# Chunk 0 ranked by token tile, its first blocks behind 12 of 16 scatters, and another written order of the head

## The chip, the cores and the metric

The kernel runs on 1 core of one Trainium2 chip. The metric is the device time of one execution in microseconds, lower is better. The kernel before was run three times: 1276.65, 1286.84 and 1290.79 us, median 1286.84 us.

## The reference

A causal 7-tap convolution along the sequence, one softmax-normalised set of taps for each of 8 heads, is followed by a mixture of 8 experts in which every token goes to the one expert with the largest logit. The input is 8 x 3584 tokens of width 192; an expert is 192 -> 1024 -> 192 with a ReLU.

```python
w = exp(weight - max) ; w = w / (sum(w) + 1e-9)            # (8 heads, 7 taps)
x = einsum('hk,bskhg->bshg', w, unfold(pad(x)))            # causal, then (28672, 192)
xn, en = x / (|x| + 1e-6), expert_emb / (|expert_emb| + 1e-6)
logits = xn @ en.T / tau
expert_idx = argmax(logits, axis=1)
gate_w = softmax(logits)[expert_idx]
out[mask_e] = gate_w[mask_e, None] * (relu(x[mask_e] @ w1[e]) @ w2[e])
```

## The kernel before, in words

The 28672 tokens are cut into 16 chunks of 1792. A chunk lies in SBUF as 112 partitions by 16 token tiles: tile t holds 112 tokens in a row, one to a partition. A chunk passes these steps:

- `load_x` fetches it; eight `conv` matmul pairs make the heads and ScalarE copies each back (L434).
- `square` sums the squares of a token tile (ScalarE L443 or VectorE L446); `scales` and `factor` turn them into a power of two and a norm.
- `scaled` works on a quarter of the chunk (4 tiles): VectorE multiplies by the power of two (L507), ScalarE casts the high half to float16 (L512, L513). `rest` subtracts to get the low half (L519, L522).
- The rows are turned so that the width lies on the partitions: for chunks 0 and 1 with TensorE transposes (`flip`, copied by ScalarE at L562), for the others with DMA transposes of SBUF by `turn` (L722), four to a chunk.
- `logits` multiplies with the expert embeddings. `rank` takes the largest logit, and finds for each token its place in its expert's region of a DRAM buffer `rows_d`. `put` scatters one token tile a time with an indirect DMA from GpSimd (L728), 16 to a chunk.

In `rank` places run first along the tiles of a partition (the scan at L657), then over the partitions (the matmuls at L667 and L669). So the first 128 places of an expert are filled from all 16 tiles.

An expert block takes 128 to 512 rows of one expert from `rows_d` with two DMA transposes (`rows_of`, L858): 40 matmuls for the hidden layer (L1002), ScalarE's ReLU to float16 (L1006), VectorE's low half (L1008), 24 matmuls for each 128 rows of output (L1023), ScalarE's scaling by the gate (L1028), an indirect store from GpSimd (L1030). The weights of all experts are first loaded, measured by `trace` and `exponents` (L355, L358, L365), and split into a high half (`high`, ScalarE L388) and a low half (`low`, VectorE L392).

The program has two parts. The head prepares the weights, takes chunks 0 and 1 to their scatters, chunk 2 up to the turned rows, and runs eight first blocks of 128 rows, one of each expert, on rows of chunk 0. Its order is written out by hand in `HEAD`, a string of short words, each of which emits one step; the instructions of TensorE, VectorE, ScalarE and GpSimd are then chained in that order (in `run`, from L1153 on), and SyncE's queue follows the program too. The words that matter here: `0k1 0k2 0k3 0u` are the four parts of chunk 0's ranking, the last with its scatters; `2s1` and `2r1` are `scaled` and `rest` of quarter 1 of chunk 2; `T2` the four DMA transposes of chunk 2; `dh3`, `dl3` the high and low halves of a part of expert 3's weights; `z6p0 z6p1 z6o` the two halves of the hidden layer and the output of expert 6's first block, `z6m` its gate; `FA` and `FB` the loads of the first blocks' rows (`first_rows`); `hx1` a trace of expert 7's weights.

Behind the head a planner (`dispatch`, `steer`) mixes expert blocks with the routing of the further chunks. The first blocks of this part are the 256-row blocks of phase 2, which need all scatters of chunks 0 and 1; `fetch` loads three of them right behind the head, and its transposes follow the four of `T2` on SyncE's queue.

`first_rows` waits for the first 16 scatters:

```python
self.after(self.rows_of(e * self.cap, v, 128, NT), NT)
```

Of the kernel before, what the change touches and what calls it, by code (L numbers as in the profile page):

```python
# [12 lines left out]
F16 = mybir.dt.float16  # L13
F32 = mybir.dt.float32
BF16 = mybir.dt.bfloat16
I32 = mybir.dt.int32
AF = mybir.ActivationFunctionType
ALU = mybir.AluOpType
AX = mybir.AxisListType
# [7 lines left out]
E = 8  # L27
F = 1024
HALO = 16
TP = 112  # L30
NT = 16
CT = TP * NT
XD = 224
RW = 240
# [18 lines left out]
NACT = 3  # L53
PINS = 12
WARM = 14
TURN, RANK, GAP = 7.0, 10.0, 0.5
RAW = 2 * (2 * F + F * D // 128)
AREAS = (1, 2), (1, 1), (1, 0), (0, 1), (1, 1), (1, 0), (0, 1)
HEAD = ("0c2 0c1 0c7 0c3 0c0 0c5 0c6 0c4 0q1 0q5 0q4 0q7 ax1 0q2 0q6 ax2 ax3 0q0 ah3 "
# [12 lines left out]
AHEAD = 0.4  # L72
HALF = 3 * 2048
SETTLE = 6.0
# [32 lines left out]
class _Moe:  # L107
# [100 lines left out]
    def constants(self):  # L208
        nc, cp = self.nc, self.cp
        nc.gpsimd.memset(self.xtb[:].rearrange(  # L210
            "p h (a k t) -> p (h a) k t", k=4, t=TP)[:, :, 3, 0:HALO], 0.0)
        nc.gpsimd.memset(self.rows2[:, :, :, XD + 2:], 0)
        nc.gpsimd.iota(self.ids, pattern=[[TP, NT]], base=TP - 1,
                       channel_multiplier=-1)
        head = self.xr[:, 0:2048].bitcast(F32)
        self.idf, self.onef = head[:, 0:128], head[:, 128:256]
        make_identity(nc, self.idf)
        self.idh = head[:, 256:320].bitcast(F16)
        nc.vector.tensor_copy(out=self.idh, in_=self.idf)
        nc.gpsimd.memset(self.onef, 1.0)  # L220
        self.oneh = cp.tile([128, 128], F16, name="oneh")
        nc.gpsimd.memset(self.oneh, 1.0)

        self.lth = cp.tile([128, 128], F16, name="lth")
        nc.gpsimd.memset(self.lth, 1.0)
        nc.gpsimd.affine_select(
            out=self.lth, in_=self.lth, pattern=[[1, 128]], base=0,
            channel_multiplier=-1, compare_op=ALU.is_gt, fill=0.0)

        tmp = self.op.tile([128, D], F32, tag="y", name="tmp")[:, 0:2 * E + 64].bitcast(I32)  # L230
        e8i = tmp[0:TP, 0:E]
        nc.gpsimd.iota(e8i, pattern=[[-1, E]], base=E, channel_multiplier=0)
        self.e8 = cp.tile([TP, E], F32, name="e8")
        nc.vector.tensor_copy(out=self.e8, in_=e8i)

        self.rst = cp.tile([TP, E, NT], F32, name="rst")
        nc.gpsimd.memset(self.rst, 1.0)
        nc.gpsimd.memset(self.rst[:, :, 0:1], 0.0)

        rn = tmp[:, E:E + NJ]  # L240
        nc.gpsimd.iota(rn, pattern=[[128, NJ]], base=1, channel_multiplier=1)
        self.rn = cp.tile([128, NJ], F32, name="rn")
        nc.vector.tensor_single_scalar(out=self.rn, in_=rn, scalar=float(self.N),
                                       op=ALU.mult)

        cbi = tmp[:, E + 64:]
        nc.gpsimd.iota(cbi, pattern=[[self.cap, E]], base=0, channel_multiplier=0)
        self.cb = cp.tile([128, E], F32, name="cb")
        nc.vector.tensor_copy(out=self.cb, in_=cbi)

        self.start = cp.tile([128, E], F32, name="start")
        nc.vector.tensor_copy(out=self.start, in_=cbi)
# [366 lines left out]
    def rank(self, c, lg, f):  # L619
        nc, sp = self.nc, self.sp  # L620
        head = c < PICK[0]
# [12 lines left out]
        if head:  # L634
# [11 lines left out]
            out=l, in0=l, scalar=0.0, op0=ALU.is_equal,  # L646
            in1=self.e8[:].unsqueeze(1).to_broadcast([TP, NT, E]), op1=ALU.mult)
        nc.vector.tensor_reduce(out=m, in_=l, op=ALU.max, axis=AX.X)
        oh = sp.tile([TP, E, NT], F32, tag="eb", name="oh")
        te = lambda v: v.rearrange("p e t -> p t e")  # L650
        nc.vector.tensor_tensor(out=te(oh[:]), in0=l, in1=bt(m[:]),
                                op=ALU.is_equal)


        inc = self.lp.tile([TP, E, NT], F32, tag="ea", name="inc")
        fl = lambda v: v.rearrange("p e t -> p (e t)")
# [32 lines left out]
        if c and c + 1 in PHASES and c + 1 < self.nch:  # L689
            self.hand_out(c + 1)  # L690


    def put(self, step=None):
        if not self.pend:
# [60 lines left out]
            self.scatter(p[:, e:e + 1], z)  # L755


    def limits(self, c):
        nc, n = self.nc, PHASES[c]
        t = self.lp.tile([128, E], F32, tag="ph_t", name="ph_t")  # L760
        nc.vector.tensor_tensor(out=t, in0=self.cb, in1=self.start, op=ALU.subtract)
        lim = self.hp.tile([128, E, NJ], F32, tag="lim", name="lim")[:, :, 0:n // 128]
        sh = [128, E, n // 128]
        nc.vector.scalar_tensor_tensor(
            out=lim, in0=t[:].unsqueeze(2).to_broadcast(sh), scalar=-float(self.N),
            in1=self.rn[:, 0:n // 128].unsqueeze(1).to_broadcast(sh),
            op0=ALU.mult, op1=ALU.add)
        at = None
        if c > 1:
            at = self.hp.tile([1, E], I32, tag="at", name="at")  # L770
            nc.vector.tensor_copy(out=at, in_=self.start[0:1, :])
        nc.vector.scalar_tensor_tensor(
            out=self.start, in0=self.start, scalar=float(n), in1=self.cb,
            op0=ALU.add, op1=ALU.min)
        self.lims[c] = lim, at

# [93 lines left out]
    def first_rows(self, k):  # L870
        nc = self.nc
        if not k:
            self.mt0 = self.cp.tile([128, E, 2], I32, name="mt0")
            m = self.rows_d[0:128, XD:XD + 2]
            self.after([nc.sync.dma_start(out=self.mt0, in_=bass.AP(
                tensor=m.tensor, offset=m.offset,
                ap=[[RW, 128], [RW * self.cap, E], [1, 2]])).ins], NT)
            self.x0 = []
        for i in range(4):
            e = 4 * k + i  # L880
            v = self.xr[:, 2048 + e * 512:2048 + (e + 1) * 512].rearrange("p (k t) -> p k t", t=128)
            self.after(self.rows_of(e * self.cap, v, 128, NT), NT)
            self.x0.append(v)

    def masked(self, ids, lim, name, behind=None):
# [350 lines left out]
```

## Time and profile before

| what | value |
| --- | --- |
| median of three runs | 1286.84 us |
| the profiled execution's own time | 1291.4 us |
| its span, first to last instruction | 1289.7 us |
| mean granted TensorE clock | 0.954 |
| TensorE matmuls busy | 1151.0 us, 89% of the span |
| VectorE, ScalarE, GpSimd busy | 665.5, 604.3, 530.0 us |

The profile is one execution. PE is TensorE's matmuls, PEld its weight loads, DVE VectorE, ACT ScalarE, POOL GpSimd, SP SyncE, which does nothing but issue DMAs. A line such as L1002 is a line of the kernel before. In a timeline row the first number is the start in us from the span's first instruction, the second the length in us; a bracket gives the idle time ahead of it and what ended that. "Issue" is time in which an engine waited for nothing that the profile shows, "remote" a signal whose sender the profile can't name. A clock of 1.00 is the upper of TensorE's two levels (2.4 GHz), 0.50 the lower (1.2 GHz).

### The profile page before, as it was taken

Reading aid. Unit: us, or ns where it says so; the run is one execution under the profiler, and the core shown is the slowest. Engines: PE = TensorE matmul, PEld = TensorE weight load, DVE = VectorE, ACT = ScalarE, POOL = GpSimd, SP = SyncE. Lnnn points to the kernel's source line nnn. Section 1 sums busy time; section 2 is a strip of 40 time slices with the busy share of each in tenths; the row PEclk is TensorE's granted clock in tenths of the full one; section 3 lists DMA queues with packets and bytes.
Section 4 is the critical chain, followed back from the end, with each engine's and each line's share of the span. In section 5 each row is a group of like instructions: output and inputs, shape, how many; then the busy total and the mean of one; then the engine's idle time right before and its main releaser. Section 6 shows DMA issues by size and latency. Waiting matters only on the chain. (4 is left out here: it accounts for less than half of the span.)

```text
span 1289.7 us, 29765 instructions
## 1 busy us (share of the span) xinstructions
PE 1151.0 (89%) x11202; PEld 905.3 (70%) x11202; DVE 665.5 (52%) x1863; ACT 604.3 (47%) x1479; POOL 530.0 (41%) x551
## 2 busy tenths in 40 slices
PE   5774998798998989899998999868999999999997
PEld 3473877586876766677776777636787878778776
DVE  5973666366545365454654737434334344445543
ACT  5973566345545545456454645213434343333333
POOL 3544245544553455355454544574222222222222
PEclk8896999899998999899999999978999999999999
DMA  9955755874966864748577574432022213221210
GB/s 250 260 115 159 144 93 137 168 160 97 183 128 149 173 124 130 169 107 185 109 159 148 121 145 103 113 87 70 29 48 51 58 39 65 65 53 33 52 45 23
DMA packets 324793, 146.64 MB, mean 114 GB/s; under 512 B 266606, under 2 KB 315117, under 8 KB 324640
## 3 DMA queue, kind: packets, MB, share of 16 engines
q1 hardware_dynamic: 300976, 93.98, 37.5%
q0 software_dynamic: 23664, 50.68, 13.6%
q8 instruction: 89, 1.46, 0.5%
q14 instruction: 64, 0.52, 0.1%
HBM read 38.35 MB, written 51.05 MB: 69 GB/s over the span
## 5 line engine op out<-in xcount | busy, mean ns | idle before, releaser
L1008 DVE SCALAR_TENSOR_TENSOR work<-h_ps,work 128x384 f16<-128x384 f32 (+1 forms) x536 | 320.0, 606 | 457.0 <-ACT work L1006 389.4
L1023 PEld LDWEIGHTS <-work 128*128 128x128 f16 x5472 | 462.6, 99 | 100.5 <-issue 47.9
L1023 PE MATMUL o_ps<-res,work 128*128 128x192 f16 x4992 | 472.0, 250 | 42.8 <-issue 23.0
L1002 PEld LDWEIGHTS <-res 128*128 128x128 f16 x3520 | 309.8, 99 | 202.0 <-issue 56.9
L1030 POOL DMA_INDIRECT out_dram<-y,id x208 | 215.4, 1036 | 455.9 <-ACT y L1028 400.2
L1006 ACT ACTIVATE work<-h_ps 128x384 f16<-128x384 f32 (+1 forms) x536 | 276.9, 533 | 245.0 <-PE h_ps L1002 176.2
L1002 PE MATMUL h_ps<-xr,res 128*128 128x384 f16 (+3 forms) x2280 | 333.7, 300 | 29.9 <-issue 22.4
L728 POOL DMA_INDIRECT rows_d<-rows,di x256 | 265.2, 1036 | 174.2 <-ACT work L1006 91.5
L1028 ACT ACTIVATE y<-o_ps,g 128x192 f32<-128x192 f32 x228 | 93.6, 418 | 253.9 <-PE o_ps L1023 152.2
L1002 PE MATMUL h_ps<-work,res 128*128 128x384 f16 (+2 forms) x1240 | 171.6, 290 | 6.8 <-issue 6.6
L431 PE MATMUL conv_ps<-xt,band 128*112 128x384 f32 x256 | 109.2, 521 | 7.0 <-issue 3.9
L434 ACT COPY xt<-conv_ps 112x384 f32<-112x384 f32 x128 | 60.5, 478 | 93.9 <-PE conv_ps L431 48.2
L443 ACT ACTIVATE sq<-xt 112x192 bf16<-112x192 f32 x196 | 70.6, 360 | 3.9
L1030 POOL DMA_INDIRECT out_dram<-y,e_mt x20 | 25.1, 1254 | 91.5 <-ACT y L1028 91.5
L512 ACT CAST rows<-xt 112x768 f16<-112x768 f32 x64 | 50.1, 828 | 20.7 <-DVE rows L510 16.9
L507 DVE TENSOR_TENSOR xt<-xt,x_p_s 112x768 f32<-112x768 f32 x64 | 58.4, 951 | 0.1
L1023 PE MATMUL o_ps<-work 128*128 128x192 f16 x480 | 46.7, 246 | 6.8 <-DVE work L850 3.3
L431 PEld LDWEIGHTS conv_ps<-xt,band 128*112 128x112 f32 x256 | 40.0, 186 | 17.9 <-issue 8.6
L1002 PE MATMUL h_ps<-xr,work 128*128 128x128 f16 x800 | 50.0, 219 | 0.3 <-issue 0.3
L513 ACT CAST rows<-xt 112x256 f16<-112x256 f32 x64 | 25.8, 405 | 48.8 <-DMA rows_d<-rows,di 34.4
L1002 PEld LDWEIGHTS <-work 128*128 128x128 f16 x800 | 46.6, 98 | 0.6 <-issue 0.4
L519 DVE TENSOR_TENSOR rows<-xt,rows 112x512 f16<-112x512 f32 x64 | 43.8, 684 | 5.1 <-ACT rows L512 5.0
(174 smaller groups left out, 601.9 us busy)
## 6 DMA issues: line engine op xcount, KB each, us to landing
xt<-in_dram SPq DMA_DIRECT2D x8, 1536.0 KB
xt<-in_dram SPq DMA_DIRECT2D x7, 1440.0 KB
res<-in_dram SPq DMA_DIRECT2D x6, 768.0 KB
rows_d<-rows,di POOLq DMA_INDIRECT x256
out_dram<-y,id POOLq DMA_INDIRECT x208
res<-in_dram SPq DMA_DIRECT2D x5, 512.0 KB
xr<-rows_d SPq DMA_TRANSPOSE x154
work<-in_dram SPq DMA_DIRECT2D x3, 512.0 KB
```

The costliest lines, as they stand in the source:

```text
L431: self.behind(nc.tensor.matmul(out=ps, lhsT=self.band[h], rhs=xt[:, :, h * G:(h + 1) * G], start=True, stop=True))
L434: nc.scalar.copy(out=xt[0:TP, :, h * G:(h + 1) * G], in_=ps)
L443: nc.scalar.activation(out=sq, in_=xc[:, t, :], func=AF.Square, accum_out=n2[:, t:t + 1])
L507: self.nc.vector.tensor_tensor(out=xc[:, u, :], in0=xc[:, u, :], in1=sb, op=ALU.mult)
L512: self.nc.scalar.copy(out=rows[:, u, 128:128 + D], in_=xc[:, u, :])
L728: i = self.nc.gpsimd.indirect_dma_start(out=self.rows_d[:, :], out_offset=bass.IndirectOffsetOnAxis(ap=idx, axis=0), in_=src, in_offset=No ...
L1002: mm = nc.tensor.matmul(out=ps[:, c, :], lhsT=wa[:, o:o + 128], rhs=xT[:, k, :], start=(i == 0), stop=(i == 4))
L1006: self.step = nc.scalar.activation(out=hh[:, b:b + m, :], in_=ps, func=AF.Relu).ins
L1008: self.last = nc.vector.scalar_tensor_tensor(out=hl[:, b:b + m, :], in0=ps, scalar=0.0, in1=hh[:, b:b + m, :], op0=ALU.max, op1=ALU.subtra ...
L1023: mm = nc.tensor.matmul(out=o, lhsT=h[:, c, q], rhs=w2[:, c, k:k + D], start=(i == 0), stop=(i == len(parts) - 1))
L1028: self.step = nc.scalar.activation(out=y, in_=o, func=AF.Copy, scale=g[:, a:a + 1]).ins
L1030: i = nc.gpsimd.indirect_dma_start(out=self.out[:, :], out_offset=bass.IndirectOffsetOnAxis(ap=ids[a], axis=0), in_=y, in_offset=None, bou ...
```

## The change

Three things change.

Chunk 0 is ranked by token tile. `rank` leaves for chunk 0 after the one-hot matrix, which is now written as float16 over all 16 tiles, and goes on in a new function `by_tile`. Two matmuls of 128 columns give, for every tile and expert, the place within the tile and the tile's total. VectorE puts the running base in column 0, ScalarE copies the totals out of PSUM, one scan over 128 partitions by 136 elements makes the running starts of all tiles, and places follow from an add, a multiply, a reduce and a cast. Tile t's tokens now lie ahead of those of tile t+1 in every expert's region.

The loads of the first blocks wait for 12 scatters (`SOON`) instead of 16, and `limits` for phase 1 works with the counts after tile 12.

`HEAD` has the same 233 words in another order. `T2` stays the last step with DMAs; one line of the string before and now:

```diff
-        "z5m 2q7 z2o 2p 2s3 gx2 2s0 z4m 2r3 2r0 X3 z3p0 z3p1 2s2 hx2 2s1 2r2 2r1 z3o "
+        "z6p0 hl2 z6p1 2s1 z6o 2r3 2r1 z7m z7p0 z7p1 T2 z7o")
```

```diff
+SOON = 12
...
+        self.early = [head[:, 320 + i * 136:456 + i * 136].rearrange(
+            "p (e t) -> p e t", e=E) for i in range(3)]
+        self.ohh = head[0:TP, 728:792].bitcast(F16).rearrange("p (e t) -> p e t", e=E)
...
+        if not c:
+            nc.vector.tensor_tensor(out=te(self.ohh), in0=l, in1=bt(m[:]),
+                                    op=ALU.is_equal)
+            yield 2.0, 0.2
+            yield from self.by_tile(r32)
+            return
...
+    def by_tile(self, r32):
+        nc, sp = self.nc, self.sp
+        fl = lambda v: v.rearrange("p e t -> p (e t)")
+        rst, tot, run = self.early
+        pc = self.ps("l", [128, 2, E, NT], F32, "pc_ps")
+        for i, w in enumerate((self.oneh, self.lth)):
+            nc.tensor.matmul(out=fl(pc[:, 1 - i]), lhsT=w[:TP, :], rhs=fl(self.ohh),
+                             start=True, stop=True)
+        nc.vector.tensor_copy(out=tot[:, :, 0], in_=self.cb)
+        nc.scalar.copy(out=tot[:, :, 1:], in_=pc[:, 1])
+        nc.vector.tensor_tensor_scan(out=fl(run), data0=fl(rst), data1=fl(tot),
+                                     initial=0.0, op0=ALU.mult, op1=ALU.add)
...
+        yield 1.7, 0.3
+        self.limits(1, run[:, :, SOON])
+        nc.vector.tensor_copy(out=self.cb, in_=run[:, :, NT])
+        self.pend += [(0, di[:, t:t + 1], r32[:, t, 0:RW]) for t in range(NT)]
+        while self.pend:
+            self.put()
...
-            self.after(self.rows_of(e * self.cap, v, 128, NT), NT)
+            self.after(self.rows_of(e * self.cap, v, 128, SOON), SOON)
```

Three places show how instructions move. First, ScalarE around chunk 0's ranking. `ex` is the exponential of the logits, `conv_ps` copies belong to chunk 1, `res<-res,w_s` is a high half of weights, `sq` a square. Before:

```order
L388 ACTIVATE res<-res,w_s 128x1024
L434 COPY xt<-conv_ps 112x16x24
L633 ACTIVATE ex<-l 112x128
L434 COPY xt<-conv_ps 112x16x24 x7
L388 ACTIVATE res<-res,w_s 128x8x192
L443 ACTIVATE sq,n_624<-xt 112x192 x10
```

With the change:

```order
L441 COPY xt<-conv_ps 112x16x24 x2
L640 ACTIVATE ex<-l 112x128
L441 COPY xt<-conv_ps 112x16x24 x3
L395 ACTIVATE res<-res,w_s 128x8x192
L441 COPY xt<-conv_ps 112x16x24 x2
L714 COPY xr<-pc_ps 128x8x16
L450 ACTIVATE sq,n_619<-xt 112x192 x10
```

The copy at L714 is new; it stands behind five convolution copies and one high half, and the scan of the ranking needs it.

Second, ScalarE ahead of and behind the first half of block 0 (`work<-h_ps`). `xtb<-tr_ps` is the copy of a flip of chunk 1. Before:

```order
L388 ACTIVATE res<-res,w_s 128x1024
L562 COPY xtb<-tr_ps 128x4x112
L434 COPY xt<-conv_ps 112x16x24
L562 COPY xtb<-tr_ps 128x4x112
L388 ACTIVATE res<-res,w_s 64x1024
L562 COPY xtb<-tr_ps 128x4x112 x3
L1006 ACTIVATE work<-h_ps 128x512 x2
L388 ACTIVATE res<-res,w_s 128x1024
L443 ACTIVATE sq,n_1098<-xt 112x192 x4
```

With the change:

```order
L395 ACTIVATE res<-res,w_s 128x8x192
L569 COPY xtb<-tr_ps 128x4x112 x2
L441 COPY xt<-conv_ps 112x16x24
L569 COPY xtb<-tr_ps 128x4x112
L1047 ACTIVATE work<-h_ps 128x512 x2
L395 ACTIVATE res<-res,w_s 128x1024
L395 ACTIVATE res<-work,w_s 128x8x192
L569 COPY xtb<-tr_ps 128x4x112 x3
```

Three flip copies and the high half `dh3` (`res<-work,w_s 128x8x192`) now stand behind block 0's first half; one convolution copy of chunk 2 (`2c1`) follows a little later.

Third, VectorE at the steps `2s1`, `2r3` and `2r1` (`xt<-xt,x_p_s` is `scaled`, `rows_92<-xt,rows_92` is `rest`, `work<-h_ps,work` the low half of a first block, one row for each half of its hidden layer). Before, where blocks 3 and 4 run:

```order
L1008 SCALAR_TENSOR_TENSOR work<-h_ps,work 128x512 x2
L507 TENSOR_TENSOR xt<-xt,x_p_s 112x768
L358 SCALAR_TENSOR_TENSOR w_dg,w_acc<-tr_ps,xr 128x128
L507 TENSOR_TENSOR xt<-xt,x_p_s 112x768
L519 TENSOR_TENSOR rows_92<-xt,rows_92 112x4x128
L522 TENSOR_TENSOR rows_92<-xt,rows_92 112x4x64
L519 TENSOR_TENSOR rows_92<-xt,rows_92 112x4x128
L522 TENSOR_TENSOR rows_92<-xt,rows_92 112x4x64
L366 TENSOR_SCALAR wexp<-n_ps 128x2
```

With the change, where blocks 6 and 7 run, the last rows of the head:

```order
L1049 SCALAR_TENSOR_TENSOR work<-h_ps,work 128x512
L399 SCALAR_TENSOR_TENSOR res<-work,w_s,res 64x1024
L1049 SCALAR_TENSOR_TENSOR work<-h_ps,work 128x512
L514 TENSOR_TENSOR xt<-xt,x_p_s 112x768
L526 TENSOR_TENSOR rows_92<-xt,rows_92 112x4x128
L529 TENSOR_TENSOR rows_92<-xt,rows_92 112x4x64
L526 TENSOR_TENSOR rows_92<-xt,rows_92 112x4x128
L529 TENSOR_TENSOR rows_92<-xt,rows_92 112x4x64
L989 TENSOR_SCALAR g_98<-mt_967,w_si 128x1
L1049 SCALAR_TENSOR_TENSOR work<-h_ps,work 128x512 x2
```

The last `rest` that `T2` needs moves from between blocks 3 and 4 to between blocks 6 and 7. On SyncE's queue nothing changes place there: `T2`'s four transposes stand ahead of the first fetch in both kernels.

## Rows read from the trace of the kernel before

**Rows 1.** Busy time by stretch: length, PE, PEld, DVE, ACT, POOL, PE clock, DMA, GB/s.
```profile
0.00:76.00 76.00, 48.14 (x416) 33.28 (x416) 55.19 (x170) 59.64 (x131) 37.62 (x65) 0.84 0.83 228
76.00:97.00 21.00, 19.02 (x278) 17.98 (x278) 18.45 (x50) 14.10 (x44) 6.64 (x6) 0.92 0.70 137
97.00:117.00 20.00, 4.14 (x16) 1.49 (x16) 0.42 (x3) 1.56 (x3) 12.77 (x14) 0.59 0.66 203
117.00:141.00 24.00, 21.97 (x286) 20.16 (x287) 21.73 (x38) 17.02 (x26) 5.23 (x5) 0.92 0.62 110
141.00:181.00 40.00, 40.00 (x405) 34.11 (x402) 21.93 (x80) 22.41 (x62) 9.29 (x9) 1.00 0.52 104
```

**Rows 2.** Timeline of PE: the start of the first block.
```profile
76.35 0.45 PE L1002 MATMUL h_ps<-xr,res 128*128 128x128 f16 x4 [3.86 <-DMA xr<-rows_d]
77.28 3.44 PE L1002 MATMUL h_ps<-xr,res 128*128 128x128 f16 x36 [0.49 <-DMA xr<-rows_d]
```

**Rows 3.** Timeline of POOL and SP: scatters 12 and 16 of chunk 0, then `FA`.
```profile
63.92 1.00 POOL L728 DMA_INDIRECT rows_d<-rows,di  x1 [0.30 <-issue]
...
69.75 1.64 POOL L728 DMA_INDIRECT rows_d<-rows,di  x1 [0.31 <-issue]
...
73.58 11.15 SPq L858 DMA_TRANSPOSE xr<-rows_d  x8
```

**Rows 4.** Timeline of DVE and ACT around chunk 0's ranking.
```profile
39.81 0.42 DVE L657 TENSOR_TENSOR_SCAN inc<-rst,oh 112x128 f32<-112x128 f32 x1
...
41.10 0.28 DVE L677 TENSOR_TENSOR inc<-inc,off 112x128 f32<-112x128 f32 x1
...
42.15 0.17 DVE L682 TENSOR_SCALAR di<-dr 112x16 int32<-112x16 f32 x1
...
37.70 2.49 ACT L434 COPY xt<-conv_ps 112x384 f32<-112x384 f32 x6
...
40.73 1.58 ACT L388 ACTIVATE res<-res,w_s 128x1536 f16<-128x1536 f32 x1
```

**Rows 5.** Timeline of ACT ahead of the first block.
```profile
74.53 1.38 ACT L562 COPY xtb<-tr_ps 128x448 f16<-128x448 f16 x3
79.19 0.60 ACT L1006 ACTIVATE work<-h_ps 128x512 f16<-128x512 f32 x1 [3.28 <-PE h_ps L1002]
```

**Rows 6.** Waits from 85 to 125 us: total, times, longest.
```profile
DVE w_dg L358 <- remote: 20.1, 1, 20.1
```

**Rows 7.** Groups of POOL's instructions, 42 to 72 us, then 90 to 111.3 us.
```profile
L728 POOL DMA_INDIRECT rows_d<-rows,di x16 | 24.2, 1513 | 15.9 <-DVE w_dg L358 11.4 <-issue 4.6
...
L728 POOL DMA_INDIRECT rows_d<-rows,di x16 | 16.4, 1025 | 8.7 <-issue 4.3 <-DVE di L682 4.2 <-DMA rows_d<-rows,di 0.3
```

**Rows 8.** Timeline: steps `2s1` to `2r1` on DVE, then `T2` and the first fetch.
```profile
122.01 0.95 DVE L507 TENSOR_TENSOR xt<-xt,x_p_s 112x768 f32<-112x768 f32 x1
...
124.47 0.42 DVE L522 TENSOR_TENSOR rows<-xt,rows 112x256 f16<-112x256 f32 x1
...
120.39 12.93 SPq L722 DMA_TRANSPOSE xtb<-rows  x4
...
135.12 2.51 SPq L858 DMA_TRANSPOSE xr<-rows_d  x2
```

**Rows 9.** SP: one transpose of `T2`; all of L722: ns, smallest/median/largest.
```profile
124.96 1.97 SPq L722 DMA_TRANSPOSE xtb<-rows  x1
...
L722 SPq DMA_TRANSPOSE xtb<-rows x56: 1407/2480/4198, 120.4 to 804.4; - x56
```

**Rows 10.** Timeline of DVE and PE: the end of block 6, the 256-row block.
```profile
135.54 1.28 DVE L1008 SCALAR_TENSOR_TENSOR work<-h_ps,work 128x512 f16<-128x512 f32 x2
...
136.28 1.49 PE L1023 MATMUL o_ps<-res,work 128*128 128x192 f16 x16 [0.63 <-DVE work L1008]
...
141.20 1.25 PE L1002 MATMUL h_ps<-xr,res 128*128 128x256 f16 x10
143.77 0.82 PE L431 MATMUL conv_ps<-xt,band 128*112 128x384 f32 x2
```

More of the change, by code (lines that the diff above doesn't have):

```diff
@@ L58 @@
 AREAS = (1, 2), (1, 1), (1, 0), (0, 1), (1, 1), (1, 0), (0, 1)
-HEAD = ("0c2 0c1 0c7 0c3 0c0 0c5 0c6 0c4 0q1 0q5 0q4 0q7 ax1 0q2 0q6 ax2 ax3 0q0 ah3 "
[12 rows of a table removed]
+HEAD = ("0c3 0c1 0c4 0c5 0c0 0c7 0c6 0c2 0q5 0q4 0q3 ax1 0q7 ax2 0q6 0q1 0q2 ax3 0q0 "
[12 rows of a table added]
 AHEAD = 0.4
@@ L228, in constants @@
             channel_multiplier=-1, compare_op=ALU.is_gt, fill=0.0)
+        self.early = [head[:, 320 + i * 136:456 + i * 136].rearrange(
+            "p (e t) -> p e t", e=E) for i in range(3)]
+        self.ohh = head[0:TP, 728:792].bitcast(F16).rearrange("p (e t) -> p e t", e=E)
+        nc.gpsimd.memset(self.early[0], 1.0)
+        nc.gpsimd.memset(self.early[0][:, :, 0:1], 0.0)
         tmp = self.op.tile([128, D], F32, tag="y", name="tmp")[:, 0:2 * E + 64].bitcast(I32)
@@ L648, in rank @@
         nc.vector.tensor_reduce(out=m, in_=l, op=ALU.max, axis=AX.X)
-        oh = sp.tile([TP, E, NT], F32, tag="eb", name="oh")
         te = lambda v: v.rearrange("p e t -> p t e")
+        oh = None if not c else sp.tile([TP, E, NT], F32, tag="eb", name="oh")
+        if not c:
[4 more added lines that the diff above has]
+            return
         nc.vector.tensor_tensor(out=te(oh[:]), in0=l, in1=bt(m[:]),
@@ L690, in rank @@
             self.hand_out(c + 1)
+    def by_tile(self, r32):
[10 more added lines that the diff above has]
+                                     initial=0.0, op0=ALU.mult, op1=ALU.add)
+        inc = self.lp.tile([TP, E, NT], F32, tag="ea", name="inc")
+        nc.vector.tensor_tensor(out=inc, in0=pc[0:TP, 0], in1=run[0:TP, :, 0:NT],
+                                op=ALU.add)
+        nc.vector.tensor_tensor(out=inc, in0=inc, in1=self.ohh, op=ALU.mult)
+        dr = sp.tile([TP, NT], F32, tag="dr", name="dr")
+        nc.vector.tensor_reduce(out=dr, in_=inc.rearrange("p e t -> p t e"),
+                                op=ALU.add, axis=AX.X)
+        di = sp.tile([TP, NT], I32, tag="di", name="di")
+        nc.vector.tensor_copy(out=di, in_=dr)
+        yield 1.7, 0.3
[4 more added lines that the diff above has]
+            self.put()
     def put(self, step=None):
@@ L755, in pads, with limits @@
             self.scatter(p[:, e:e + 1], z)
-    def limits(self, c):
+    def limits(self, c, have=None):
         nc, n = self.nc, PHASES[c]
+        have = self.cb if have is None else have
         t = self.lp.tile([128, E], F32, tag="ph_t", name="ph_t")
-        nc.vector.tensor_tensor(out=t, in0=self.cb, in1=self.start, op=ALU.subtract)
+        nc.vector.tensor_tensor(out=t, in0=have, in1=self.start, op=ALU.subtract)
         lim = self.hp.tile([128, E, NJ], F32, tag="lim", name="lim")[:, :, 0:n // 128]
@@ L772, in limits @@
         nc.vector.scalar_tensor_tensor(
-            out=self.start, in0=self.start, scalar=float(n), in1=self.cb,
+            out=self.start, in0=self.start, scalar=float(n), in1=have,
             op0=ALU.add, op1=ALU.min)
@@ L876, in first_rows @@
                 tensor=m.tensor, offset=m.offset,
-                ap=[[RW, 128], [RW * self.cap, E], [1, 2]])).ins], NT)
+                ap=[[RW, 128], [RW * self.cap, E], [1, 2]])).ins], SOON)
             self.x0 = []
```

22 rows, old and new, of the table HEAD are left out of this document.

## Prediction

> **What bounds the kernel now.** The page names TensorE, busy for 89% of the span, but the change touches only the head, so I read the table by stretch first [rows 1]. There the head has four characters. Up to 76 us it is the preparation: TensorE is busy for 48.14 of 76.00 us, ScalarE for 59.64 and VectorE for 55.19; the chain runs through the routing of chunk 0. From 76 to 97 us the first blocks run, TensorE busy for 19.02 of 21. From 97 to 117 us nearly everything stands: TensorE 4.14 of 20, VectorE 0.42. From 117 to 141 us the rest of the head, 21.97 of 24. Behind 141 us TensorE is busy without a gap, 40.00 of 40.00 at clock 1.00: whatever the head gains or loses in the start of the first 256-row block, the end gains or loses too.
>
> Next the timeline of TensorE at the start of block 0: at 76.35 it had waited 3.86 us for the load of the rows, and soon 0.49 more [rows 2]. GpSimd and SyncE say for what the load waited [rows 3]: the twelfth scatter ends at 63.92 + 1.00 = 64.92, the sixteenth at 69.75 + 1.64 = 71.39, the load goes out at 73.58. ScalarE too waits there, 3.28 us up to the first ReLU at 79.19 [rows 5]. So the scatters of chunk 0 do end last here, but only by about 3.5 us: what a still earlier load gains must come out of the engines' own work.
>
> For the standstill the list of waits names one wait of VectorE, 20.1 us, released by a sender that the profile can't name [rows 6]. GpSimd runs in it chunk 1's 16 scatters one behind the other, 16.4 us busy and 8.7 idle [rows 7].
>
> Last, the end of the head: `2r1` ends at 124.47 + 0.42 = 124.89, `T2` at 120.39 + 12.93 = 133.32, the fetch at 135.12 + 2.51 = 137.63 [rows 8]; the 256-row block starts at 141.20 and its row has no wait [rows 10]. So today this load is hidden, with about 3 us to spare.
>
> **A: 12 scatters instead of 16.** The gap between the two scatters is 71.39 - 64.92 = 6.5 us [rows 3]. Against it stands the ranking by tile. Its scan waits for the new copy at L714, which stands on ScalarE behind five convolution copies (2.49 / 6 = 0.415 each) and a high half (1.58). From 37.70 that is 37.70 + 5 x 0.415 + 1.58 = 41.4, and with a copy taken like a convolution copy 41.8. The scan (0.42) and the steps from the add to the cast (41.10 to 42.15 + 0.17, so 1.2) end at 43.4 to 43.5, where before they end at 42.32: 1.2 later [rows 4]. The load comes 6.5 - 1.2 = 5.3 earlier, at 68.3, and TensorE could begin at 76.35 - 5.3 = 71.1. Is another late then? ScalarE is free at 74.53 + 1.38 = 75.91 [rows 5]; the three flip copies (1.38) and `dh3` (1.58, priced by the high half [rows 4]) leave its queue ahead of the first ReLU, so 75.91 - 2.96 = 72.95. TensorE needs the first ReLU at 79.19 - 5.3 = 73.9. ScalarE is ready 0.9 before it. TensorE's own work ends at 76.35 - 3.86 = 72.49 now [rows 2]; with 0.7 less ahead of block 0 (part B) that is 71.8, and it has idle time further up to give, so at most 0.7 of the gain is at risk here. A gains 5.3; the bounds are 0 (something else holds the loads) and 6.5.
>
> **B: work moved behind block 0.** Nothing is dropped: what goes out ahead of block 0 comes back behind it. The flips (12 transposes), the two convolution matmuls of `2c1` and 12 logit matmuls go behind, one trace of `hx1` ahead: I take 0.7 us more for TensorE. The convolution pair alone is 0.82 [rows 10]; the others are small matmuls, and `hx1` gives some of it back. On VectorE `dl3` comes behind block 0, and VectorE is busy there for 18.45 of 21.00 us [rows 1], so it hides only a part: 0.8 us is my estimate. On ScalarE 14.10 of 21.00 is busy; its 3 us go into the idle time. B costs 1.5, bounds 0 and 3.0 (ScalarE's share unhidden). The head before the tail is then 5.3 - 1.5 = 3.8 earlier.
>
> **C: the standstill.** It lies in chunk 1's scatters, which run as a burst of 16 in both kernels. I take it to come back at 0. Were it gone: at the rate of the stretch before, 19.02 / 21.00 = 0.906, 20 us would hold 18.1 us of TensorE's work, and they hold 4.14 [rows 1]. (18.1 - 4.1) / 0.906 = 15.5 us. Those are the ends, 0 and -15.5.
>
> The row: chunk 0's scatters, issued while VectorE works, take 1513 ns in the mean, chunk 1's, while it stands, 1025 ns [rows 7]. The Trainium skill, "SBUF — State Buffer", section "SBUF: two separate sides", says that VectorE and GpSimd lock each other out of a shared pair of ports while TensorE's and ScalarE's own ports wait for nobody. The trace agrees on scatters beside a busy VectorE being the longer ones. By that rule a scatter burst can't in itself hold TensorE for 20 us, the standstill would be an accident of the order, and a new order may lose it; the sum would be 15.5 lower. The traced burst and standstill coincide, which speaks against it; this is the second rival.
>
> **D: `2s1`, `2r3` and `2r1` moved behind block 6.** They cost VectorE the same as before, so nothing by themselves. But the last three transposes of `T2` wait for `2r1`, and the fetch stands behind them on SyncE's queue. Count from the end of block 6's second low half (136.82 in the trace of before, 135.54 + 1.28 [rows 10]). The chain `2s1` to `2r1` takes 124.89 - 122.01 = 2.9 us [rows 8], with a small start some 3.1. From `2r1`'s end to the fetch's end it took 137.63 - 124.89 = 12.7 us, and the data come 0.9 later: in the first load the second of eight transposes (11.15 / 8 = 1.39 each) is issued by 73.58 + 2 x 1.39 = 76.37 [rows 3], and TensorE's wait ends at 77.28 [rows 2]. So the fetched block can start at 3.1 + 13.7 = 16.8.
>
> When does TensorE get there? Block 7's two low halves (1.28) follow the chain on VectorE, at 3.1 + 0.2 (its gate) + 1.3 = 4.6. From the end of the low halves to the end of the output matmuls it takes 136.28 + 1.49 - 136.82 = 0.95 [rows 10], so the head's matmuls end at 5.6. The next in the order is one convolution pair (0.82), and then the fetched block: 6.4. TensorE stands for 16.8 - 6.4 = 10.4 us, where it had no wait. Bounds: `T2`'s last three transposes took 133.32 - 124.96 = 8.4 [rows 8, 9]; at the line's smallest, 3 x 1.41 = 4.2, the gap is 6.2, at its largest, 3 x 4.20 = 12.6, it is 14.6 [rows 9]. I take 10.4, since it is the same four transposes in the same company.
>
> **E: the clock.** Behind the standstill of 97 to 117 us the granted clock of the 24 us that follow is 0.92, against 1.00 in the 40 us after that [rows 1]: 24 x 0.08 = 1.9 us. A gap of 10 us brings, by that row, up to the same; I take 2.0, bounds 0 and 3.
>
> **Sum.** -5.3 + 1.5 + 0 + 10.4 + 2.0 = +8.6 us. The profiled execution took 1291.4 us (a span of 1289.7 and 1.7 around it), so it would come to 1300.0; it lies 4.6 above the median of the runs shown, so I set the sum on the median: 1286.84 + 8.6 = 1295.4. With D's bounds, and half of the others', the forecast's own range is about 1290 to 1301.
>
> **The rivals.**
>
> First, `T2` and the fetch are hidden anyway: VectorE reaches `2s1` early, or other work stands behind the head for TensorE to do. For it: 3 us of slack today [rows 8, 10]. Against it: the three rests stand behind block 6's low halves in VectorE's written order, and the slack is below the 10.4. D and E fall away: 1286.84 - 5.3 + 1.5 = 1283.0.
>
> Second, the standstill doesn't come back. For it: chunk 0's scatters also come 16 to a chunk, from 42 to 72 us, and bring no such standstill [rows 7]. Against it: chunk 1's burst is the same in the new order. 1295.4 - 15.5 = 1279.9. With the first rival as well, 1283.0 - 15.5 = 1267.5.
>
> Third, on the slower side: A gains nothing. Its place is the first ReLU of block 0, its price the 5.3 us. The copy at L714, the only new instruction of ScalarE, holds the ranking longer than I count, or the weights for block 0 are what is late. It decides from the point where the ReLU starts no earlier than 79.19: 1286.84 + 1.5 + 10.4 + 2.0 = 1300.7. For it: ScalarE is the fullest engine up to 76 us, 59.64 of 76.00 [rows 1]. Against it: its 3.28 us of idle time just ahead of this ReLU [rows 5] and the 2.96 us of work taken out.
>
> That the change doesn't do what it says would need the wait for 12 scatters to be ended by another step; that is the third rival too.
>
> **How the numbers follow.** The forecast gets 0.48: each of its terms is a count of moved instructions with durations from rows. The first rival gets 0.13, the second 0.18, both together 0.06, the third 0.15. About 1% is what a measurement of this kernel can tell from no change: 1274.0 and 1299.7. Below 1274.0 lies the pair of rivals (0.06), and as much again for the second rival's and the unknown case's lower tails: 0.12. Above 1299.7 lie nearly all of the third rival (0.13) and a quarter of the forecast, whose upper end is 1301 (0.13): 0.26. Between them 0.62. The range of 8 in 10 leaves out the pair and the tails of D above 14 us: 1277 to 1304.
>
> **What would show it.** In the profile of the changed kernel: TensorE's first block starts near 71 instead of 76.35 and the wait for `xr<-rows_d` there is small (A; if it starts behind 75 A is wrong). A standstill of some 20 us again covers chunk 1's scatters (C). The last `rest` on VectorE stands behind block 6, `T2`'s last transposes and the fetch follow it by some 13 us, and TensorE waits about 10 us for `xr<-rows_d` ahead of the first 256-row block (D); a wait under 5 us there makes the forecast wrong, and so does a wait that was in the head anyway. Behind that gap the clock is below 1.00 for a stretch (E). If TensorE is gapless from 105 us on, the second rival holds.

## The result, and the profile after

The changed kernel takes 1291.73 us (median of 11 runs, 1285.07 to 1302.41), the kernel before in the same comparison 1283.3 us (median of 11, 1276.65 to 1290.79). The ratio is 1.0062, 95% interval 1.0041 to 1.0084: 5 to 11 us slower, 8 us by the middle. The forecast was +8.6 us, to 1295.4.

The profiled execution took 1293.36 us, only 2 us more than the profiled one of before. That difference says little: both executions stand still at several places of the main part too, at other moments and for other lengths. The head, where the change is, can be read place by place, and it is read so here.

First the page of the changed kernel: TensorE's row, its 40 slices and its clock.

```profile
PE 1144.8 (89%) x11202; PEld 906.5 (70%) x11202; DVE 667.5 (52%) x1862; ACT 606.7 (47%) x1480; POOL 535.1 (41%) x553
...
PE   5785698778898999899998999959999999999997
...
PEclk8897799889998999899999999979999999999999
```

Of the change nothing shows at this grain but that slices 4 and 5 are emptier than those around them; slice 27 is one of the standstills of the main part. The table by stretch, cut where the changed kernel's stages lie, answers to [rows 1] (length, PE, PEld, DVE, ACT, POOL, clock, DMA, GB/s):

```profile
71.00:95.00 24.00, 21.01 (x333) 20.01 (x330) 21.33 (x55) 20.74 (x58) 13.55 (x19) 1.00 0.75 138
95.00:120.00 25.00, 9.64 (x96) 9.12 (x97) 8.77 (x20) 7.75 (x12) 13.99 (x14) 0.67 0.59 166
120.00:141.00 21.00, 13.69 (x179) 12.06 (x177) 15.62 (x34) 9.50 (x16) 5.73 (x5) 0.91 0.43 78
141.00:160.00 19.00, 14.41 (x139) 11.80 (x140) 2.90 (x6) 4.28 (x9) 1.95 (x2) 0.72 0.58 133
160.00:181.00 21.00, 21.00 (x208) 17.89 (x205) 11.51 (x44) 12.85 (x38) 2.26 (x3) 1.00 0.49 84
```

The first blocks start by 71 instead of 76 us. The standstill is back: TensorE is busy for 9.64 of the 25 us from 95 to 120. What is new is the hole on both sides of 141 us, and the clock of 0.72 behind it, where the kernel before had 40.00 of 40.00 at 1.00.

Now the timelines, each in order of its engine. The start of block 0 on TensorE, the twelfth and sixteenth scatter on GpSimd (64.28 and 69.89 are their ends), and the first of the loads, which answer to [rows 2, 3]:

```profile
69.70 0.39 PE L1043 MATMUL h_ps<-xr,res 128*128 128x128 f16 x4
70.75 2.17 PE L1043 MATMUL h_ps<-xr,res 128*128 128x128 f16 x36 [0.66 <-DMA xr<-rows_d]
...
63.03 1.25 POOL L768 DMA_INDIRECT rows_d<-rows,di  x1 [0.30 <-issue]
...
68.35 1.54 POOL L768 DMA_INDIRECT rows_d<-rows,di  x1 [0.30 <-issue]
...
66.50 1.30 SPq L899 DMA_TRANSPOSE xr<-rows_d  x1
```

The load goes out between the two, 7.1 us earlier than before (66.50 against 73.58), and TensorE starts 6.65 us earlier (69.70 against 76.35) after 0.66 us of waiting where there were 3.86 and 0.49.

The end of the head, which answers to [rows 8, 10]: VectorE's last low half of block 6 and the last `rest`, TensorE's block 7 and the first 256-row block, SyncE's `T2` and fetch, and last a row of SyncE's waits from 95 to 146 us (total, times, longest).

```profile
128.96 0.69 DVE L1049 SCALAR_TENSOR_TENSOR work<-h_ps,work 128x512 f16<-128x512 f32 x1
129.57 0.95 DVE L514 TENSOR_TENSOR xt<-xt,x_p_s 112x768 f32<-112x768 f32 x1
...
132.02 0.42 DVE L529 TENSOR_TENSOR rows<-xt,rows 112x256 f16<-112x256 f32 x1
...
132.55 2.23 PE L1064 MATMUL o_ps<-res,work 128*128 128x192 f16 x24
134.62 0.82 PE L438 MATMUL conv_ps<-xt,band 128*112 128x384 f32 x2
145.59 4.87 PE L1043 MATMUL h_ps<-xr,res 128*128 128x256 f16 x22 [10.15 <-DMA xr<-rows_d]
...
98.20 41.82 SPq L762 DMA_TRANSPOSE xtb<-rows  x4
142.21 2.52 SPq L899 DMA_TRANSPOSE xr<-rows_d  x2
...
SPq L762 <- DVE rows L529: 35.4, 2, 30.3
```

Read from the bottom: TensorE waits 10.15 us for the rows that the fetch of 142.21 brings; the fetch stands behind `T2`, which ends at 98.20 + 41.82 = 140.02; `T2` stands for most of its 41.82 us, since its second transpose needs the `rest` (L529) that ends at 132.44: the list of waits puts 30.3 us in one piece down to it. On VectorE that `rest` stands, as written, behind block 6's low half.

What the gap leaves behind is the clock (the same table, cut finer, and the row of the block's other 18 matmuls):

```profile
145.00:150.00 5.00, 4.41 (x21) 3.15 (x22) 0.00 (x0) 0.00 (x0) 0.00 (x0) 0.50 0.37 64
150.00:160.00 10.00, 10.00 (x120) 8.65 (x118) 2.90 (x6) 4.28 (x9) 1.95 (x2) 0.93 0.72 183
...
150.62 2.54 PE L1043 MATMUL h_ps<-xr,res 128*128 128x256 f16 x18
```

TensorE works again from 145.59 on, but at the lower of its two levels until behind 150 (granted clock 0.50 up to 151 us, 1.00 from 152). The 22 matmuls of 4.87 us take 2.5 at the rate of the 30 that run in 3.44 us in the run rest_early below (0.115 us each): 2.35 us lost. The 18 behind them lose 0.5 more, 2.54 us where that rate gives 2.06.

### The profile page after: what moved, and what is told of

It is laid out like the page before. It is cut to its first block, busy times and chain, and to the rows that moved or that the text cites. A ratio compares the mean times of both kernels' runs of the same rounds, so it can differ in the third digit from the quotient of the medians.

```text
span 1291.6 us, 29773 instructions
## 1 busy us (share of the span) xinstructions
PE 1144.8 (89%) x11202; PEld 906.5 (70%) x11202; DVE 667.5 (52%) x1862; ACT 606.7 (47%) x1480; POOL 535.1 (41%) x553
## 5 line engine op out<-in xcount | busy, mean ns | idle before, releaser
L1064 PEld LDWEIGHTS <-work 128*128 128x128 f16 x5472 | 464.4, 99 | 119.5 <-issue 53.1
L1043 PE MATMUL h_ps<-xr,res 128*128 128x384 f16 (+3 forms) x2280 | 328.9, 300 | 21.2 <-DMA xr<-rows_d 10.8
L752 PEld LDWEIGHTS <-xtb 128*128 128x128 f16 x768 | 29.0, 98 | 25.8 <-DMA xtb<-rows 12.6
```

Source lines behind the costliest of these rows:

```text
L1043: mm = nc.tensor.matmul(out=ps[:, c, :], lhsT=wa[:, o:o + 128], rhs=xT[:, k, :], start=(i == 0), stop=(i == 4))
L1064: mm = nc.tensor.matmul(out=o, lhsT=h[:, c, q], rhs=w2[:, c, k:k + D], start=(i == 0), stop=(i == len(parts) - 1))
```

## The experiments

Eleven runs in three groups, each group on one chip. In the first group the kernel before takes 1284.83 us (26 runs), in the other two 1207.61 and 1205.99: the same program, 6% faster. So times are compared within a group, as ratios to before; across groups I compare only ratios and places in the head.

**The tail, put back.** The changed kernel with three words moved forward again:

```diff
-"... 2s2 2s3 2r0 hx2 2r2 z6m z4p0 ... z6p0 hl2 z6p1 2s1 z6o 2r3 2r1 z7m z7p0 z7p1 T2 z7o"
+"... 2s2 2s3 2r0 hx2 2r2 2s1 2r3 2r1 z6m z4p0 ... z6p0 hl2 z6p1 z6o z7m z7p0 z7p1 T2 z7o"
```

> The changed kernel, with 2s1, 2r3 and 2r1 back behind 2r2, ahead of block 4. Theory (D and E are real): in the changed kernel TensorE waits 10.15 us for the fetched rows ahead of the first 256-row block; here 2r1 ends some 12 us earlier on VectorE, the fetch is ready before TensorE is, the wait is under 1 us, the first 256-row block starts near 136 instead of 145.59, and with the slow clock behind the gap (1.7 us) the time is about 12 us below the changed kernel's 1291.7: 1280, ratio to before 0.997. Rival (the gap only moves: the fetch waits for chunk 1's scatters or something else that ends late): a wait of 8 us or more stays, the time stays near 1291, ratio 1.006.

Measured: 1279.72 us, ratio 0.9970 (0.9946 to 0.9995), 12 us below the changed kernel of the first result (11.8 by the ratios). The wait is gone (no bracket behind the row), and the block starts at 134.54:

```profile
134.54 1.25 PE L1043 MATMUL h_ps<-xr,res 128*128 128x256 f16 x10
137.92 3.44 PE L1043 MATMUL h_ps<-xr,res 128*128 128x256 f16 x30
```

The three words alone turn a kernel that is slower than before into one that is faster. The theory holds, the rival falls.

**The tail alone, in the kernel before.** The other direction, with nothing else of the change:

```diff
-"... 2s0 z4m 2r3 2r0 X3 z3p0 z3p1 2s2 hx2 2s1 2r2 2r1 z3o ... z6p0 z6p1 hl2 z6o z7m T2 ..."
+"... 2s0 z4m 2r0 X3 z3p0 z3p1 2s2 hx2 2r2 z3o ... z6p0 z6p1 hl2 2s1 z6o 2r3 2r1 z7m T2 ..."
```

> The kernel before, with only 2s1, 2r3 and 2r1 moved behind block 6, as in the changed kernel. Theory: D and E alone, a wait of 10 to 12 us ahead of the first 256-row block where there was none, and about 2 us of slow clock behind it: 1283.3 + 12 = 1295, ratio 1.009. Rival (the gap comes from the rest of the new order, as the block ends being earlier): the wait is below 5 us and the ratio under 1.004.

Measured: 1299.19 us, ratio 1.0111 (1.0076 to 1.0146), with the wait ahead of the first 256-row block:

```profile
155.42 4.05 PE L1002 MATMUL h_ps<-xr,res 128*128 128x256 f16 x22 [9.09 <-DMA xr<-rows_d]
```

The gap is 0.9 us under the expected 10 to 12, the time within its interval. So the gap needs nothing of the rest of the new order.

**Sixteen scatters instead of twelve.** The changed kernel with the old wait, for the rows and for their tokens' numbers:

```diff
-                ap=[[RW, 128], [RW * self.cap, E], [1, 2]])).ins], SOON)
+                ap=[[RW, 128], [RW * self.cap, E], [1, 2]])).ins], NT)
...
-            self.after(self.rows_of(e * self.cap, v, 128, SOON), SOON)
+            self.after(self.rows_of(e * self.cap, v, 128, NT), NT)
```

> The changed kernel, but the loads of the first blocks wait for all 16 scatters. Theory (A is worth what the scatters lie apart): the 12th scatter ends at 64.28 and the 16th at 69.89 in the changed kernel, so block 0 starts 5.6 us later, at about 75.3, and the whole head with it; time 1291.7 + 5.6 = 1297, ratio 1.0107. Rival (A is absorbed by the standstill in chunk 1's scatters, which ends when these end): block 0 starts later, but the first 256-row block stays within 2 us of 145.6 and the time within 2 us of 1291.7, ratio 1.006.

Measured: 1294.87 us, ratio 1.0078 (1.0043 to 1.0113), and on TensorE:

```profile
75.59 4.45 PE L1043 MATMUL h_ps<-xr,res 128*128 128x128 f16 x40 [4.84 <-DMA xr<-rows_d]
...
149.84 4.15 PE L1043 MATMUL h_ps<-xr,res 128*128 128x256 f16 x22 [9.57 <-DMA xr<-rows_d]
```

Block 0 starts 5.9 us later than in the changed kernel (75.59 against 69.70), as the theory says, the 256-row block 4.25 later. The time lies between the two expectations, and its interval holds both: inconclusive on what A is worth at the end.

**A alone.** The kernel before in its own order of `HEAD`, with the ranking by tile and the twelve scatters:

```diff
+SOON = 12
...
+            yield from self.by_tile(r32)
...
-            self.after(self.rows_of(e * self.cap, v, 128, NT), NT)
+            self.after(self.rows_of(e * self.cap, v, 128, SOON), SOON)
```

> The kernel before in its own written order, with chunk 0 ranked by tile and the first loads behind 12 scatters: A alone. Theory (A is worth what block 0 gains): block 0 starts 5 to 7 us earlier, at 70 to 71 instead of 76.35, and time falls by 5 to 6 us: 1278, ratio 0.996. Rival (a part of A is taken back before the 256-row block, as in wait_16, where block 0 came 7.8 us later and the 256-row block only 4.3): block 0 is 5 us or more earlier, the 256-row block 0 to 3 us, ratio 0.998 to 1.001. If ScalarE's new copy eats A, block 0 starts later than 74 and the ratio is 1.000 or above.

Measured: 1202.92 us, ratio 0.9960 (0.9942 to 0.9978). Block 0 starts at 72.55 in this profile (70 to 71 expected), and the first 256-row block has no wait. (The expectation's 7.8 us for block 0 in wait_16 is not its start, which came 5.9 us later.) It was run once more:

> A alone once more. Where before is near 1208: ratio 0.996 again. Where before is near 1284: the load of the first 256-row block is hidden, and the 256-row block comes 3 to 6 us earlier than the kernel before's 141.2, ratio 0.995 to 0.998; rival (the standstill takes A back), the 256-row block comes within 1.5 us of 141.2, ratio 0.999 to 1.001.

Measured: 1204.81 us, ratio 0.9975 (0.9952 to 0.9998). Both intervals lie below 1: 3 to 5 us by the middles. Block 0 starts at 73.62 in the second profile. A is a gain, near the 5.3 of the forecast or somewhat below. The case of a chip with before near 1284 did not come.

**The standstill: scatters apart, first attempt.** The changed kernel with chunk 1's scatters cut into four parts in the written order (`HEAD` has the word `1u` three times more, behind `z3o`, `z4o` and `z5o`):

```diff
         while head and self.pend:
             self.put()
+            if c and len(self.pend) in (4, 8, 12):
+                yield
```

> The changed kernel, with chunk 1's 16 scatters in four groups of 4, behind blocks 2, 3, 4 and 5 instead of one burst. Theory (the standstill between 95 and 117 us is made by the burst): TensorE's busy share of that stretch rises from 0.39 to over 0.75, the head ends 8 to 15 us earlier, time 1277 to 1284, ratio 0.995 to 1.000. Rival (the standstill comes from the load of x that is going on at the same time, or from the amount of scatters and not from their being in one burst): the same microseconds are lost, 15 in all, time within 3 us of 1291.7, ratio 1.006.

Measured: 1289.2 us, ratio 1.0006 (0.9976 to 1.0036), the standstill as long as ever:

```profile
95.00:120.00 25.00, 11.10 (x124) 10.48 (x123) 10.43 (x22) 9.20 (x15) 13.72 (x15) 0.73 0.60 174
```

It tests nothing: these scatters are not chained in the written order, and 13 of the 16 still ran in front of block 3's output, with one output between them. The lower ratio I can't explain from the head, where the 256-row block starts only 2.4 us earlier.

**Scatters apart, with waits,** on top of rest_early; only GpSimd's order differs from it (`1u` stands three times more in `HEAD`, behind `z2o`, `z3o` and `z4o`):

```diff
-            self.put()
+            n = len(self.pend)
+            self.put(self.step if c and n < 13 else None)
+            if c and n in (5, 9, 13):
+                yield
```

> rest_early, with chunk 1's 16 scatters held apart by waits: 4 at once, 4 behind block 2's scaled output, 4 behind block 3's, 4 behind block 4's. The other engines' orders are unchanged. (In the run called split only three scatters had moved away from the burst, so it didn't test this.) Theory (the standstill is made by many scatters back to back): TensorE's busy share from 95 to 120 us rises from 0.44 to over 0.75, the first 256-row block starts at 120 to 128 us instead of 134.5, time 6 to 14 us below rest_early's 1279.7: 1266 to 1274. Rival (each scatter costs TensorE the same wherever it stands, or the standstill has another cause): TensorE loses some 14 us in the same blocks, the block starts within 2 us of 134.5 or later, time 1278 or more.

**The load of chunk 3 later,** also on top of rest_early: the word `X3` moved behind `T2`.

> rest_early, with the load of chunk 3 (1.5 MB, in flight from about 93 to 104 us, where the standstill begins) moved behind T2. Theory (burst of scatters): the standstill stays, TensorE busy for 10 to 13 of the 25 us from 95 to 120, and chunk 3's convolutions, which now wait for the load, cost some us at 134 to 145: time 1280 to 1290. Rival (the load's traffic makes the standstill): TensorE busy for over 18 of the 25 us.

Measured, in the second group: split_waits 1207.63 us, ratio 1.0015 (0.9992 to 1.0039), and x3_late 1210.94 us, ratio 1.0027 (0.9999 to 1.0055). TensorE's busy time from 95 to 120 us is 19.07 and 19.68 of 25. But by_tile_alone, which has the plain burst of 16 scatters and the load of chunk 3 in its old place, shows the same there:

```profile
95.00:120.00 25.00, 20.22 (x275) 18.96 (x273) 21.89 (x40) 17.03 (x26) 18.67 (x18) 0.95 1.06 250
```

In this group there is no standstill to take away, so neither edit was tested against it. None of these kernels was profiled in the first group, so this alone does not acquit the written order; after_again, next, is the same program in both.

**The third group** put the changed kernel, rest_early, split_waits and A alone on one chip. It ran on the chip with the number 13, as the first group did; the second group ran on number 6.

> The changed kernel once more, beside rest_early, split_waits and by_tile_alone on one chip. On the chip of the second group of runs the kernel before took 1207.6 us, and its kernels showed no standstill from 95 to 117 us. Theory (the standstill is a trait of the chip, the gap of D is not): on a chip with before near 1284 the ratio is 1.006 again, standstill 14 us or more; on one with before near 1208 there is no standstill, the gap ahead of the first 256-row block is again 9 to 11 us, and the ratio is 1.004 to 1.010. Rival (the gap needs the standstill): without a standstill the gap is under 5 us and the ratio at most 1.000.

Measured: 1213.27 us against 1205.99, ratio 1.0057 (1.0031 to 1.0083). The rows of the standstill's stretch and of the 256-row block:

```profile
95.00:120.00 25.00, 18.94 (x246) 18.28 (x246) 19.46 (x29) 15.76 (x24) 17.63 (x18) 0.86 0.65 186
...
132.78 4.88 PE L1043 MATMUL h_ps<-xr,res 128*128 128x256 f16 x22 [9.64 <-DMA xr<-rows_d]
```

No standstill, 18.94 of 25 us where the same program showed 9.64 in the first result, and the same gap, 9.64 us, with the same slow 22 matmuls behind it. The gap does not need the standstill, and the change costs as much without it. The standstill is not made by the written order alone. Nor is it a trait of the chip, as the expectation had it: number 13 shows it in the first group and not in this one.

> rest_early once more. Theory: where before is near 1284, ratio 0.997 again. Where before is near 1208, chunk 1's scatters (POOL, until 118 to 121 us) end last instead of T2, TensorE waits 3 to 6 us for the fetched rows, and the ratio is 0.998 to 1.003, 5 us or so under the changed kernel. Rival: it stays 12 us under the changed kernel on either chip.

Measured: 1203.3 us, ratio 0.9980 (0.9959 to 1.0001), 10.0 us under the changed kernel:

```profile
121.37 0.61 PE L1043 MATMUL h_ps<-xr,res 128*128 128x256 f16 x4 [1.40 <-DMA xr<-rows_d]
```

The ratio is in the expected range, the wait is not: 1.40 us instead of 3 to 6. In the second group's split_waits it was 4.76, in x3_late 0.32, so it varies. The distance to the changed kernel is nearer to the rival's 12 than to my 5: I had the end of chunk 1's scatters too late (the last starts at 110.87 here).

> split_waits once more. Only where before is near 1284 does it test the burst: theory, the standstill is made by the scatters' back-to-back run on such a chip, so TensorE is busy for over 18 of the 25 us from 95 to 120, ratio 0.986 to 0.993; rival, it loses 14 us as in rest_early, ratio 0.996 or more. Where before is near 1208, nothing stands still and the ratio is within 0.002 of rest_early's.

Measured: 1207.81 us, ratio 1.0003 (0.9976 to 1.0030); 0.0023 from rest_early's, with intervals that overlap. Holding the scatters apart brings nothing where nothing stands still; where something does, it was not tried.

So two versions beat both kernels, by little: A alone (0.9960 and 0.9975 of the kernel before) and rest_early (0.9970 and 0.9980, the second interval just reaching 1). Both keep the ranking by tile and leave out the new tail.

## Why the prediction was right, step by step

The time came out at +8 us against +8.6, and by the road that was forecast: a gain ahead of block 0, more than given back by a gap ahead of the first 256-row block. Term by term:

**A was 1.35 us too small, and not all of what came is A's.** Forecast 5.3 earlier, measured 6.65. The ranking ended when I said, at 43.40 (43.4 to 43.5), but the releaser was another than I named. VectorE and ScalarE around the ranking, which answers to [rows 4]:

```profile
40.04 1.28 DVE L399 SCALAR_TENSOR_TENSOR res<-res,w_s 64x1024 f16<-64x1024 f32 x1
41.36 0.17 DVE L713 COPY xr<-cb 128x8 f32<-128x8 f32 x1
41.64 0.44 DVE L715 TENSOR_TENSOR_SCAN xr<-xr 128x136 f32<-128x136 f32 x1
...
43.23 0.17 DVE L725 CAST di<-dr 112x16 int32<-112x16 f32 x1
...
40.65 0.28 ACT L714 COPY xr<-pc_ps 128x128 f32<-128x128 f32 x1
```

ScalarE's copy ended at 40.93, 0.9 earlier than worked out; the scan started at 41.64, behind a low half and a copy on VectorE's own queue. Two errors of the working cancelled. What made A larger lay behind it: the scatters ran faster. The 16 took 21.6 us, 1351 ns in the mean, where they had taken 1513 [rows 7]:

```profile
L768 POOL DMA_INDIRECT rows_d<-rows,di x16 | 21.6, 1351 | 16.7 <-DVE w_dg L365 12.1 <-issue 4.6
```

That goes with the new order of `HEAD` and not with the ranking by tile. From the first scatter's start to the twelfth's end it took 20.6 us in all nine profiles of the new order (43.70 to 64.28 in this one), and 22.0 in both profiles of A alone, which keeps the old order; the kernel before took 22.3. Why the new order does it is not shown. At 69.70 itself no wait stands: the load was ready, and TensorE's own work ended last there.

**B came out on the other side, and through a term that the prediction did not have.** Before, 16 of block 7's 24 output matmuls stood behind the 256-row block's first ten:

```profile
140.53 0.83 PE L1023 MATMUL o_ps<-res,work 128*128 128x192 f16 x8
...
142.44 1.49 PE L1023 MATMUL o_ps<-res,work 128*128 128x192 f16 x16
```

Without the 1.24 us of the block ahead of them (142.44 - 141.20) the head's own matmuls end at 142.44 + 1.49 - 1.24 = 142.69, so 66.3 us after block 0's start. Now it is 132.55 + 2.23 - 69.70 = 65.1: 1.3 us less, where I had 1.5 more. Block 0 itself makes the difference: its last 36 matmuls took 3.44 us before [rows 2], at a granted clock of 0.61, and take 2.17 now, at 1.00. That is 1.27 us; the prediction priced the clock behind D's gap only. In wait_16 and before_rest_late, behind waits of 4.84 and 3.10 us, block 0's 40 matmuls are slow again, 4.45 us at 0.50 in the first; but in x3_late they take 4.13 us behind a wait of 0.76, so the wait ahead is not the only cause. The moved work by itself then cost about nothing in these two executions, but both stretches hold the standstill, whose length may differ by more than that. The nearest the times come to B is rest_early, which is the change without its tail, against A alone in the third group: 0.9980 against 0.9975, 0.6 us, with intervals that overlap. So B's size stays open.

**C was right for the pair that was compared, and its reason is open.** From 95 to 120 us TensorE was busy for 9.64 us with the change and for 8.80 before:

```profile
95.00:120.00 25.00, 8.80 (x72) 5.77 (x71) 4.87 (x17) 3.67 (x7) 14.23 (x15) 0.61 0.61 184
```

But the argument for it, that the standstill coincides with chunk 1's burst, does not carry: by_tile_alone has the same burst and 20.22 of 25. The Trainium skill, "SBUF — State Buffer", section "SBUF: two separate sides", says that TensorE's way to SBUF never waits on another engine. That row agrees. So the second rival was right that the burst is no cause in itself, and wrong in what follows: with the same order the standstill comes in one execution (9.64 of 25 us busy) and not in another (18.94). With it or without, the change costs 0.6%. The prediction's reading of [rows 7], that scatters beside a busy VectorE are the longer ones, does not hold up either: in by_tile_alone chunk 1's 16 ran beside a VectorE that was busy for 22.09 of 22.56 us and took 1124 ns in the mean, much nearer to the 1025 of the standstill than to the 1513 of chunk 0.

**D was right within 0.3 us,** and so were its parts. From block 6's last low half (128.96 + 0.69 = 129.65) to the end of the last `rest` (132.44) it took 2.8 us (forecast 3.1); from there to the end of the fetch (144.73) 12.3 (12.7); the data came 0.86 later (0.9). TensorE got through block 7 and one convolution pair at 134.62 + 0.82 = 135.44, 5.8 behind the low half (6.4). The gap: 10.15 us (10.4), and 9.09 to 9.64 us in the four other profiles with the same tail (before_rest_late, wait_16, split and after_again). The first rival, a fetch that is hidden anyway, falls with these rows.

**E:** 2.35 us on the block's first 22 matmuls and 0.5 on the other 18, 2.8 in all; 2.0 forecast. In the four other profiles with the tail the same 22 took 4.05 to 4.88 us, so the price of the clock varies by 0.8 us.

**The sum** up to the 256-row block, counted from the end of the head's own work before (142.69): -6.65 - 1.3 + 0.7 (the convolution pair, which now stands ahead of the block) + 10.15 = +2.9, which is 145.59 - 142.69. The slow clock adds 2.8, and the pair is given back behind the block: +5.1 in these two executions, against the forecast's 8.6. So A and B together were forecast 4.1 us too dear (1.35 and 2.8), E 0.8 too cheap. The runs give 5 to 11 us; the forecast is nearer to their middle than to this pair, and part of that is luck, since single executions differ by more than this error.

**The third rival** (A gains nothing) falls with block 0 at 69.70.

## What to carry to other kernels

A queue that issues in order turns a late producer of its first entry into a late start of everything behind it: before moving a step to the end of a written order, look for the DMA that reads its result and for what stands behind that DMA on its queue. Count the slack from the moved instruction itself (here 13 us from the end of the last `rest` to the fetched block, against 3 us of TensorE's work in the same time), not from the step that is named as last. Here the gap on TensorE cost more than its length: 2.8 us of slow matmuls behind 10.15 us of waiting.

## What was not expected of the hardware

The same program took 1284.83 us in one group of runs and 1207.61 and 1205.99 us in the others. The profiles show where most of it lies. This is TensorE's costliest group of instructions, in the changed kernel of the first result and then of the third group, whose spans are 79 us apart (busy, mean ns, then the idle time ahead and its causes):

```profile
L1064 PE MATMUL o_ps<-res,work 128*128 128x192 f16 x4992 | 473.8, 250 | 60.4 <-issue 26.0 <-ACT work L1047 23.0 <-DVE work L1049 10.3
```

```profile
L1064 PE MATMUL o_ps<-res,work 128*128 128x192 f16 x4992 | 453.5, 247 | 23.2 <-DVE work L1049 14.1 <-ACT work L1047 9.0
```

The group's idle time is 37 us less in the second and its busy time 20 us less. The 26.0 us of "issue", time in which TensorE waited for nothing that the profile shows, are gone, and with them part of its waits for ScalarE. In the standstill it is ScalarE whose wait has no named sender (the waits from 85 to 121 us in the changed kernel: total, times, longest):

```profile
ACT work L1047 <- remote: 16.6, 2, 10.7
DVE work L1049 <- ACT work L1047: 10.6, 1, 10.6
```

TensorE's 40 matmuls for these two ReLUs stand in the trace as ended at 101.78 (ends of matmuls are modelled); ScalarE starts the two at 104.27 and 115.61. TensorE was busy for 8.58 to 11.10 of the 25 us from 95 to 120 in all six profiles of the first result and the first group, and for 18.43 to 20.22 in all seven of the others. The first and the third group ran half an hour apart on the chip with the same number, so another chip is not the answer there (that of the first result is not known). What differed, and what held TensorE and its signals up in the first, stays open. No edit aimed at it was tested where it occurs, except split, which did not take the scatters apart.
